# Attention with forgetting gates and a SwiGLU block on one core: first loads in another order, two PSUM banks kept for the first products with v, and all units planned anew

## The chip, the cores and the metric

The kernel runs on one core of a Trainium2 chip. The metric is the device time of one execution in microseconds (us); the time before is the median of three runs, 419.12 us. A trace of one further execution shows what each engine did: PE (TensorE, matmuls; PEld are its weight loads), DVE (VectorE), ACT (ScalarE), POOL (GpSimd) and SP (SyncE, which here only issues DMAs). ACT and POOL issue DMAs too, each on a queue of its own.

## What is computed

Eight batches with eight heads, 576 positions, head size 64. Attention with a decay from cumulated logarithms of the gates f, causal, and then a gated feed-forward block on the joined heads (4608 tokens, 512 wide, inner width 1536). Cut to what matters:

```python
scores = q @ k.T / sqrt(64)
cum = cumsum(log(clip(f, 1e-4, 1)), axis=-1)
scores = where(causal, -1e9, scores + cum[:, :, :, None] - cum[:, :, None, :])
attn = softmax(scores) @ v
x = attn.transpose(0, 2, 1, 3).reshape(4608, 512)
g = x @ w_gate
out = (g * sigmoid(g) * (x @ w_val)) @ w_out
```

q, k, v, f and the weights come as float32 from HBM; matmuls run in bfloat16, sums in float32.

## The kernel before

**Units.** Two heads that lie beside each other make a pair: 32 pairs, four to a batch, 0 to 3 for batch 0. A pair's nine blocks of 64 queries fall into group 0 (blocks 0 to 3) and group 1 (blocks 4 to 8). A unit is a pair and a group, written 10 for pair 1, group 0. `HEAD` (L266) orders the first eight units: 00 10 20 30 11 01 31 21.

**What one unit does.** `scores` (L581): matmuls of a pair's q (tile qz, which is the stationary operand) with its k (kt) into banks of the pool sp (two banks), with a small mask matmul (L598). DVE adds the cumulated gates (tile cb) and takes the row minimum in the same pass (L622), into one of four t tiles. ACT takes exp with row sums (L642). DVE inverts the sums (L658 or ACT's L656, then L660), POOL, or ACT in the early units, scales (L678, tile pk). For pairs 0 to 7 PE transposes pk (L708), and DVE or ACT copy the result to pT (L713); later pairs use a DMA transpose. `weighted` (L716) multiplies pT with v (L734, "PV") into a bank of the pool tx (two banks), and `spread` copies that to the token-major operand xT (L758).

**q and k.** They are loaded as f32 rows, cast to bf16 (tiles qb, kb), transposed on PE into a bank of the same pool tx (L546; later pairs L467), and copied to qz and kt (L559, L561). For pairs 0 to 3 this is done in parts: part A holds the first 256 positions, which is all that group 0 needs, part B the other 320. `parts` (L486) makes one load group for two pairs: k A, q A and k B for pairs 0 and 1 together, the same for pairs 2 and 3, and q B for each pair. `load_parts` (L493) issues a group as two DMAs where it holds two pairs. Part A of pairs 0 and 1 is issued by ACT (L507), all else by SP.

**Gates of the attention.** The 64 rows of f are loaded as one tile (`gates`, L365): DVE clips (L370), ACT takes Ln (L372), DVE scans (L373). The result goes to HBM as cum_f (L382), and each pair's rows are read back from it, copied to 64 partitions (cb). For the first parts of pairs 0 to 3 and the second part of pair 0 a matmul with a 0/1 matrix does the copying instead (`select`, L389, PE's L395, copied by DVE or ACT at L400). A dummy activation (L384) makes ACT load the table that holds exp.

**The feed-forward block.** Tokens are taken in tiles of 256, 256, seven of 512, 256, 128 and 128. `gate` (L801): matmuls of xT with w_gate and w_val into banks of the pool gv (four banks, also used for the transposes of pk, the selects and the output), ACT's tanh (L822), two products on DVE (L824, L827). `project` (L830): matmuls with w_out (L844), a copy (L851) and the store (L856). A gate unit needs xT of all four pairs of its batch. POOL issues the loads of the weights in 11 pieces (L791, L795): gate and val in columns 0 to 255, 256 to 511, 512 to 1023, 1024 to 1535, then w_out in three.

**What sets the order.** The kernel records each operation with the engines that may run it, an assumed duration, the tiles it reads and writes and a priority. `Plan.order` (L63) is a list scheduler that runs when the kernel is built: it takes again and again the operation that can start first by its own clock, breaking ties by priority, and gives it an engine and a buffer. Its result is one fixed order for every engine's queue; on the chip each queue runs in that order and waits where data or a buffer isn't ready. So an assumed duration, or a wait that only the planner knows (`after`), changes nothing but the order, the engine and the buffer. `COLD` (L17) is the planner's time until which it doubles PE's durations. `STARTUP` (L265) lists the loads of the start in their order: f9 is f, p0 and p2 are parts A of two pairs, k and q parts B, c the rows of cum_f, v01 chunk 1 of batch 0's v, wg0 the piece of w_gate that begins at column 0 (numbers in blocks of 128), p4 and up whole pairs. Each load waits in the plan for the one `AHEAD` places before it, POOL's also for the one `BEHIND` places before. `NUDGE` (L269) moves the priorities of single units: a are attention units, f gate tiles, o output tiles, q preparations of a pair, v loads of v.

Of the kernel before, what the change touches and what calls it, by code (L numbers as in the profile page):

```python
# [11 lines left out]
ALU = mybir.AluOpType  # L12
# [1 line left out]

BIG = 1.0e9
HUGE = 3.0e38
COLD = 25000  # L17
SLOW = 1.03


# [179 lines left out]
def kernel(  # L200
# [11 lines left out]
    nc = tc.nc  # L212
    B, H, S, D = q.shape
# [36 lines left out]
    NHALF = 4  # L250
    NSELA = 4
    NSEL = 1
    CUT = QB * (HI[0] + 1)
    MOST = (("p", 1), ("o", 2), ("f", 3))
    AHEAD = 10
    BEHIND = 6
    BOTH = 8
    LATER = {"DVE": 100}
# [3 lines left out]
    SOON = 8  # L262
    BACK = 4
    CBACK = 5
    STARTUP = "p0 f9 k0 p2 wv0 wg0 c0 v01 q1 q0 wv2 wg2 c1 v02 v00 k2 v04 c3 q2 wv4 v03 wg4 q3 c2 p4 v11 c4 wg8 wv8 c5 v14 p5 v13 v12 p6 c7 v10 c6 wo0 wo4 wo8 p7"  # L265
    HEAD = "00 10 20 30 11 01 31 21"  # L266


    NUDGE = "a5.0:-2 a8.0:1 a13.0:-1 a15.0:-2 a17.0:-2 a18.0:1.5 a22.0:2.5 a23.0:-1 a25.1:-1 a26.1:-1.5 f1:-2 f5:9 f7:0.5 o3:-4.5 o4:-0.5 o6:-8 o7:-3 q8:-2 q13:-3.5 q20:-2 q23:2 q25:4 q26:3.5 q30:-2"  # L269

    WAIT = ""
    ORDER = [(int(u[0]), int(u[1])) for u in HEAD.split()]
# [7 lines left out]
    pl = Plan()  # L280
# [79 lines left out]

    fall = f.rearrange("b h s -> (b h) s")

    evacs, loads, sums = [], {}, {}

    def gates(key, parts, np_, prio):  # L365
        x = lambda: pl.buf(key)[0:np_, :]
        for n, (a, z, src) in enumerate(parts):
            loads["f", key, n] = pl.op({"SP": 600}, lambda e, a=a, z=z, src=src: nc.sync.dma_start(out=pl.buf(key)[a:z, :], in_=src),
                                       (), [(key, 0)] + [key] * (n == 0), prio + n * .01, dma=570)
        pl.op({"DVE": 460}, lambda e: nc.vector.tensor_scalar(x(), x(), 1.0e-4, 1.0, op0=ALU.max, op1=ALU.min),  # L370
              [(key, 0)], [(key, 1)], prio, holds=[key])
        pl.op({"ACT": 690}, lambda e: nc.scalar.activation(x(), x(), AF.Ln), [(key, 1)], [(key, 2)], prio, holds=[key])  # L372
        pl.op({"DVE": 1350}, lambda e: nc.vector.tensor_tensor_scan(x(), tiny[0:np_, 0:1].to_broadcast((np_, S)), x(), 0.0, ALU.mult, ALU.add),  # L373
              [(key, 2), "tiny"], [(key, 3)], prio, holds=[key])
# [118 lines left out]
    def load_parts(p):  # L493
        b, hp = divmod(p, NPB)
        pl.key(("cb", p), "cb", p)
        for name, x, a, z, r, n in parts(p):
            fk = (name + "f", p, x)
            pl.key(fk, name + "f")
            m = (z - a) // r

            def load(e, fk=fk, src=(k if name == "k" else q), a=a, z=z, r=r, n=n, m=m):
                for u in range(n):
                    h0 = 2 * (hp + u)
                    (nc.scalar if e == "ACT" else nc.sync).dma_start(
                        out=pl.buf(fk)[m * u:m * u + m, :, 0:r * D],
                        in_=src[b, h0:h0 + 2, a:z].rearrange("h (p r) d -> p h (r d)", r=r))
            loads[name, p, x] = pl.op({"ACT" if p == 0 and x == "A" else "SP": 550 * n}, load, (), [fk], -99 + 3 * p, dma=n * (z - a) * 2)  # L507
        for x, a, z, sel in (("A", 0, CUT, NSELA), ("B", CUT, S, NSEL)):
            if p < sel:
                select(p, x, a, z)  # L510
                continue
            for h in range(2):
                loads["cb", p, x, h] = pl.op({"SP": 600}, lambda e, h=h, a=a, z=z: nc.sync.dma_start(
                    out=pl.buf(("cb", p))[64 * h:64 * h + 64, a:z],
                    in_=cum_dram[2 * p + h:2 * p + h + 1, a:z].to_broadcast((64, z - a))),
                    ["cum_dram"], [(("cb", p), x)], -98.5 + 3 * p, dma=z - a, holds=[("cb", p)])

    def prepare_parts(p):
        for name, x, a, z, r, n in parts(p):
            fk, bk, tk = (name + "f", p, x), (name + "b", p, x), ("tt", name, p, x)  # L520
            m = (z - a) // r
            pr = min(at[p + u, x == "B"] for u in range(n)) - 1 + (name == "q") * .1
            pl.key(bk, name + "b")
            pl.key(tk, "tx", line="q")

            def cast(e, name=name, fk=fk, bk=bk, r=r, w=m * n):
                src = pl.buf(fk)[0:w, :, 0:r * D].rearrange("p h (r d) -> p r h d", d=D)
                dst = pl.buf(bk)[0:w, 0:r, :, :]
                if e == "ACT":
                    nc.scalar.activation(dst, src, AF.Copy, scale=-scale if name == "q" else 1.0)  # L530
                elif name == "q":
                    eng[e].tensor_scalar(dst, src, -scale, 1.0, op0=ALU.mult, op1=ALU.mult)
                else:
                    eng[e].tensor_copy(dst, src)
            L = 2 * r * D
            o = pl.op({"POOL": L + 60, "ACT": L * .833 + 210, "DVE": L * .62 + 60}, cast, [fk], [bk], pr)
            o.bias = SPARE if p else {}
            oks = [(("kt" if name == "k" else "qz"), p + u) for u in range(n)]
            if x == "A":
                for ok in oks:  # L540
                    pl.key(ok, ok[0])

            def transpose(e, bk=bk, tk=tk, r=r, w=m * n):
                src = pl.buf(bk).rearrange("p r h d -> p r (h d)")
                for j in range(r):
                    nc.tensor.transpose(half(tk)[:, w * j:w * j + w], src[0:w, j, :], ident[0:w, 0:w])  # L546
            pl.op({"PE": r * (m * n / 2.4 + 2.5)}, transpose, [bk], [tk] + (oks if x == "A" else []), pr, lat=200, holds=oks)
            for u in range(n):
                for lo, hi, h in ([(0, P, None)] if name == "k" else [(0, 64, 0), (64, 128, 1)]):
                    def evac(e, lo=lo, hi=hi, h=h, u=u, tk=tk, ok=oks[u], a=a, z=z, r=r, n=n, m=m):  # L550
                        src = half(tk)[lo:hi, 0:r * m * n]
                        if h is None:
                            src = src.rearrange("c (j u p) -> c u p j", j=r, u=n)[:, u, :, :]
                            dst = pl.buf(ok)[lo:hi, a:z].rearrange("c (p j) -> c p j", j=r)
                        else:
                            src = src.rearrange("c (j u i p) -> c u i p j", j=r, u=n, i=(z - a) // QB)[:, u, :, :, :]
                            dst = pl.buf(ok)[lo:hi, a // QB:z // QB, h, :].rearrange("c i (p j) -> c i p j", j=r)
                        if e == "ACT":
                            nc.scalar.copy(dst, src)  # L559
                        else:  # L560
                            nc.vector.tensor_copy(dst, src)  # L561
                    pl.op({"ACT": (z - a) * .85 + 125, "DVE": (z - a) * 1.15 + 90}, evac,
                          [tk] + ([("z", "qz", p + u)] if h is not None and p + u < len(pl.pools["qz"]) else []),
                          [(oks[u], x)], at[p + u, int(x == "B")] - .9, holds=[oks[u]])
# [151 lines left out]
    def weighted(p, gs):  # L716
        b, hp = divmod(p, NPB)
        keys, cost = [], 190
        for g in gs:
            pl.key(("xo", p, g), "tx", line="v")  # L720
            w = HI[g] - LO[g] + 1
            keys.append(("xo", p, g))
            cost += mm(*[QB * min(w, HI[g] - 2 * c + 1) for c in range(HI[g] // 2 + 1)])

        def mult(e):
            for g in gs:
                xo, pT, vt = pl.buf(("xo", p, g)), pl.buf(("pT", p, g)), pl.buf(("vt", b))
                w, nch = HI[g] - LO[g] + 1, HI[g] // 2 + 1
                for c in range(nch):
                    n = min(w, HI[g] - 2 * c + 1)  # L730
                    a = w * c if (g, c) != (1, 4) else NSL[g] - 1
                    for h in range(2):
                        r = slice(64 * h, 64 * h + 64)
                        nc.tensor.matmul(xo[r, 0:QB * n], vt[:, c, 2 * hp + h, :], pT[:, a:a + n, 64 * h:64 * h + 64],  # L734
                                         start=(c == 0), stop=(c == nch - 1))
        o = pl.op({"PE": cost}, mult, [("pT", p, g) for g in gs] + [("vt", b, c) for c in range(max(HI[g] for g in gs) // 2 + 1)],
              keys, at[p, gs[0]], lat=220, holds=[("vt", b)])
        for g in gs:
            spread(p, g, o)

# [129 lines left out]
    for b in range(B):  # L870
        pl.key(("vt", b), "vt")
        load_v(b)
    weights()
    line = []
    for x in STARTUP.split():
        n = int("".join(c for c in x if c.isdigit()))
# [95 lines left out]
```

## Time and profile before

| what | us |
|---|---|
| median of three runs (417.67 to 419.34) | 419.12 |
| the profiled execution, its own time | 418.96 |
| its span, first to last instruction | 417.2 |
| PE busy | 398.3 (95%) |
| DVE busy | 328.9 (79%) |
| ACT busy | 310.3 (74%) |
| POOL busy | 251.7 (60%) |
| matmuls of the gate unit, L816 | 110.6 and 109.3 |
| matmuls of the output, L844 | 104.2 |
| score matmuls, L594 and L598 | 71.9 and 48.0 |
| DVE's add with minimum, L622 | 130.4 |
| 16 DMA engines, queue of SP, share of the span | 71.1% |
| the same, queue of POOL (weights) | 7.6% |

Shares of busy time are means over the whole span. Matmuls are pipelined and their ends are modelled in the records, so the lengths of following matmuls overlap; the distance of their starts tells their pace. The mean granted TensorE clock is 0.996. The chain of waits that ended last lies on PE for 86% of the span and on DVE for 4%.

### The profile page before, as it was taken

What the parts mean: (1) busy time and instruction counts of PE and PEld (TensorE: products, weight loads), DVE (VectorE), ACT (ScalarE), POOL (GpSimd) and SP (SyncE); (2) the same over time, 40 slices, a digit from 0 to 9 for tenths busy, and PEclk for the clock granted to TensorE, in tenths of its full rate; (3) what the DMA queues carried; (4) which work ended last, traced back from release to release, by engine and by line L of the source; (5) the groups of instructions that cost most, each with busy time, mean ns of one, the idle gap of its engine ahead of it and who ended that gap; (6) DMA issues with size and microseconds to landing.
All of it is one profiled execution on the core that took longest, in us unless ns stands there. A gap on an engine that the chain in (4) does not pass through costs nothing.

```text
span 417.2 us, 9955 instructions
## 1 busy us (share of the span) xinstructions
PE 398.3 (95%) x3250; PEld 232.3 (56%) x3296; DVE 328.9 (79%) x1065; ACT 310.3 (74%) x872; POOL 251.7 (60%) x459
## 2 busy tenths in 40 slices
PE   1979999999999999999999999999999999999996
PEld 0636878665555555555555554555555444457675
DVE  5688999999998899989897797798967764565232
ACT  4798999989995999899999984798996533232221
POOL 7589698987887897976968678267773400000000
PEclk9998999999999999999999999999999999999999
DMA  9999979695999999899999999848999211000211
GB/s 183 253 210 225 190 135 252 159 234 141 200 229 215 264 218 236 203 232 222 228 234 218 240 221 223 194 116 190 221 217 186 55 37 50 25 27 25 77 52 52
DMA packets 144004, 71.83 MB, mean 172 GB/s; under 512 B 117904, under 2 KB 131728, under 8 KB 143952
## 3 DMA queue, kind: packets, MB, share of 16 engines
q1 hardware_dynamic: 137568, 65.95, 71.1%
q0 software_dynamic: 5808, 4.72, 7.6%
q10 hardware_dynamic: 576, 0.52, 0.5%
q8 instruction: 26, 0.43, 0.4%
q14 instruction: 26, 0.21, 0.3%
HBM read 46.65 MB, written 9.58 MB: 135 GB/s over the span
## 4 chain that ended last, share of the span: by engine, by line
PE 86%; DVE 4%; issue 1%; ACT 0%
PE gv L816 43%; PE gv L844 22%; PE sp L594 9%; PE tx L734 6%; PE tx L467 3%; PE sp L598 2%; PE gv L708 2%; DVE t L622 1%; DVE pT L713 1%; DVE hh L827 1%; DVE th L824 1%; DVE qz L481 1%; DVE kt L481 0%; ACT ot L851 0%; DVE tm L622 0%
## 5 line engine op out<-in xcount | busy, mean ns | idle before, releaser
L622 DVE CUSTOM_DVE_ANT_0 t<-sp,cb 128x320 f32<-128x320 f32 (+7 forms) x288 | 130.4, 475 | 12.1 <-PE sp L598 8.6
L678 POOL TENSOR_SCALAR pk<-e,lr 128x128 bf16<-128x128 f32 (+3 forms) x190 | 100.5, 533 | 61.8 <-DVE lr L660 16.5
L816 PE MATMUL gv<-xT,wg 128*128 128x512 bf16 (+2 forms) x563 | 110.6, 327 | 0.8
L816 PE MATMUL gv<-xT,wv 128*128 128x512 bf16 (+2 forms) x562 | 109.3, 324 | 0.9
L844 PE MATMUL gv<-wo,hh 128*128 128x512 bf16 (+1 forms) x425 | 104.2, 373 | 0.8
L824 DVE SCALAR_TENSOR_TENSOR th<-th,gv 128x512 f32<-128x512 f32 x108 | 73.9, 684 | 39.3 <-ACT th L822 38.3
L822 ACT ACTIVATE th<-gv 128x512 f32<-128x512 f32 x108 | 64.1, 594 | 44.0 <-PE gv L816 43.1
L642 ACT ACTIVATE e<-t,tm 128x576 f32<-128x576 f32 (+4 forms) x160 | 88.7, 556 | 8.9 <-DVE tm L622 8.3
L827 DVE TENSOR_TENSOR hh<-th,gv 128x512 bf16<-128x512 f32 x108 | 73.7, 685 | 8.7 <-PE gv L816 4.9
L642 ACT ACTIVATE eo<-t,tm 128x128 f32<-128x128 f32 (+3 forms) x128 | 71.1, 556 | 4.7 <-DVE tm L622 2.9
L594 PE MATMUL sp<-kt,qz 128*128 128x448 bf16 (+6 forms) x320 | 71.9, 293 | 1.5 <-DVE tm L622 1.4
L678 POOL TENSOR_SCALAR pk<-eo,lr 128x128 bf16<-128x128 f32 (+3 forms) x127 | 67.6, 532 | 5.4 <-DVE lr L660 3.1
L816 PEld LDWEIGHTS <-wg 128*128 128x128 bf16 x576 | 49.8, 98 | 35.7
L816 PEld LDWEIGHTS <-wv 128*128 128x128 bf16 x576 | 48.9, 98 | 33.7 <-issue 0.3
L844 PEld LDWEIGHTS <-hh 128*128 128x128 bf16 x444 | 39.9, 98 | 39.0
L598 PE MATMUL sp<-mask,ident 128*128 128x64 bf16 x288 | 48.0, 197 | 0.0
L594 PEld LDWEIGHTS <-qz 128*128 128x128 bf16 x320 | 30.9, 100 | 20.9 <-DVE tm L622 0.9
L851 ACT ACTIVATE ot<-gv 128x512 f32<-128x512 f32 (+1 forms) x31 | 17.9, 580 | 27.1 <-PE gv L844 26.2
L598 PEld LDWEIGHTS <-ident 128*128 128x128 bf16 x288 | 27.2, 100 | 12.6 <-issue 1.9
L734 PE MATMUL tx<-pT,vt 128*64 128x320 bf16 (+4 forms) x448 | 29.6, 266 | 1.9 <-DVE pT L713 1.3
L451 POOL TENSOR_SCALAR qb<-qf 72x1024 bf16<-72x1024 f32 x28 | 29.1, 1041 | 3.1 <-DMA qf<-in_q_dram 2.0
L642 ACT ACTIVATION_READ_ACCUMULATOR e<-t,tm 128x1 f32 x160 | 30.6, 192 | 0.0
(69 smaller groups left out, 389.0 us busy)
## 6 DMA issues: line engine op xcount, KB each, us to landing
out_dram<-ot SPq DMA_DIRECT2D x35, 256.0 KB
vf<-in_v_dram SPq DMA_DIRECT2D x32, 256.0 KB
cb<-cum_f SPq DMA_DIRECT2D x56, 144.0 KB
kf<-in_k_dram SPq DMA_DIRECT2D x28, 288.0 KB
qf<-in_q_dram SPq DMA_DIRECT2D x28, 288.0 KB
wo<-in_moe_w_out_dram POOLq DMA_DIRECT2D x3, 512.0 KB, 10.8
vf<-in_v_dram SPq DMA_DIRECT2D x8, 128.0 KB
wv<-in_moe_w_val_dram POOLq DMA_DIRECT2D x2, 512.0 KB, 8.4
```

The source lines that it names most:

```text
L451: eng[e].tensor_scalar(dst, src, -scale, 1.0, op0=ALU.mult, op1=ALU.mult)
L594: nc.tensor.matmul(sp[:, o:o + z - a], qz[:, i, :, :].rearrange("p h r -> p (h r)"), kt[:, a:z], start=True, stop=not last or p >= MFROM)
L598: nc.tensor.matmul(sp[:, o - QB:o], ident, mask, start=False, stop=True)
L622: nc.vector.tensor_tensor_reduce(out=pl.buf(tk)[:, a:z], in0=pl.buf(sk)[:, o:o + z - a], in1=pl.buf(("cm", p))[:, i, :] if own else pl.buf ...
L642: nc.scalar.activation(pl.buf(ek)[:, :L], pl.buf(tk)[:, :L], AF.Exp, bias=pl.buf(("tm", p, g))[:, 0, i:i + 1], scale=-1.0, accum_out=pl.bu ...
L678: eng[e].tensor_scalar(dst, src, r, 1.0, op0=ALU.mult, op1=ALU.mult)
L734: nc.tensor.matmul(xo[r, 0:QB * n], vt[:, c, 2 * hp + h, :], pT[:, a:a + n, 64 * h:64 * h + 64], start=(c == 0), stop=(c == nch - 1))
L816: nc.tensor.matmul(pl.buf(bk)[:, j * n:j * n + n], wt[:, ko, fc * P:fc * P + P], xT[:, ko, x0:x0 + n], start=ko == 0, stop=ko == KD - 1)
L822: pl.op({"ACT": 487}, lambda e, u=u: nc.scalar.activation(pl.buf(("th", t, u)), pl.buf(("wg", t, u)), AF.Tanh, scale=0.5), [("wg", t, u)], ...
L824: pl.op({"DVE": 605}, lambda e, u=u: nc.vector.scalar_tensor_tensor(pl.buf(("th", t, u)), pl.buf(("th", t, u)), 1.0, pl.buf(("wg", t, u)), ...
L827: pl.op({"DVE": 605}, lambda e, u=u: nc.vector.tensor_mul(pl.buf(("hh", t, u)), pl.buf(("th", t, u)), pl.buf(("wv", t, u))), [("u", t, u), ...
L844: nc.tensor.matmul(pl.buf(bk)[:, 0:z - a], hh[:, (fc % nf) * n + ms * P:(fc % nf) * n + ms * P + P], wo[:, fc, a:z], start=fc == 0, stop=f ...
```

## The change

Seven edits, all in what the planner is given:

- `STARTUP`: f is listed first (it was second); p0 and p2 follow it directly, and the rest has a new order.
- Part A of q of pairs 0 and 1 is issued by SP instead of ACT; ACT keeps part A of k.
- The three transposes of parts B of pairs 2 and 3 (k of both, q of each) wait in the plan for the PV of pair 3, group 0. Those transposes and the PVs share the two tx banks.
- `AHEAD` is 9 instead of 10.
- Assumed durations: PE doubled until 31 us instead of 25; the clip of f 0.70 us instead of 0.46; an issue of a part 0.62 instead of 0.55.
- `NUDGE` is another list.

```diff
-COLD = 25000
+COLD = 31000
...
+    LASTA = 3
...
-    AHEAD = 10
+    AHEAD = 9
...
-    STARTUP = "p0 f9 k0 p2 wv0 wg0 c0 v01 q1 q0 wv2 wg2 c1 v02 v00 k2 v04 c3 q2 wv4 v03 wg4 q3 c2 p4 v11 c4 wg8 wv8 c5 v14 p5 v13 v12 p6 c7 v10 c6 wo0 wo4 wo8 p7"
+    STARTUP = "f9 p0 p2 k0 q1 wg2 v00 wv0 k2 wv2 c1 q0 wg0 v01 c3 v02 wg4 c2 v04 v03 q3 q2 wv8 p5 p4 v10 c4 wv4 c5 c0 p6 c6 wg8 c7 wo0 v14 wo8 v13 v12 p7 v11 wo4"
...
-    NUDGE = "a5.0:-2 a8.0:1 a13.0:-1 a15.0:-2 a17.0:-2 a18.0:1.5 a22.0:2.5 a23.0:-1 a25.1:-1 a26.1:-1.5 f1:-2 f5:9 f7:0.5 o3:-4.5 o4:-0.5 o6:-8 o7:-3 q8:-2 q13:-3.5 q20:-2 q23:2 q25:4 q26:3.5 q30:-2"
+    NUDGE = "a7.1:1.5 a13.1:-2 a14.0:2 a16.0:-1 a17.0:-2.5 a21.0:-2 a24.0:2 a26.0:3 f4:-1 f6:1 f8:8 o0:1 o4:-4 q2:0.5 q13:-1.5 q14:-2 q15:-4.5 q16:-4 q19:-3 q23:-3.5 q25:1.5 q27:-4 q29:-0.5 q30:-2.5 v6:2 v7:8.5"
...
-    evacs, loads, sums = [], {}, {}
+    evacs, loads, sums, lasts, heads = [], {}, {}, [], {}
...
-        pl.op({"DVE": 460}, lambda e: nc.vector.tensor_scalar(x(), x(), 1.0e-4, 1.0, op0=ALU.max, op1=ALU.min),
+        pl.op({"DVE": 700}, lambda e: nc.vector.tensor_scalar(x(), x(), 1.0e-4, 1.0, op0=ALU.max, op1=ALU.min),
...
-            loads[name, p, x] = pl.op({"ACT" if p == 0 and x == "A" else "SP": 550 * n}, load, (), [fk], -99 + 3 * p, dma=n * (z - a) * 2)
+            loads[name, p, x] = pl.op({"ACT" if (name, p, x) == ("k", 0, "A") else "SP": 620 * n}, load, (), [fk], -99 + 3 * p, dma=n * (z - a) * 2)
...
-            pl.op({"PE": r * (m * n / 2.4 + 2.5)}, transpose, [bk], [tk] + (oks if x == "A" else []), pr, lat=200, holds=oks)
+            o = pl.op({"PE": r * (m * n / 2.4 + 2.5)}, transpose, [bk], [tk] + (oks if x == "A" else []), pr, lat=200, holds=oks)
+            if x == "B" and p >= 2:
+                lasts.append(o)
...
+        heads[p, gs[0]] = o
...
+    for o in lasts:
+        o.after.append(heads[LASTA, 0])
```

The planner makes new orders of this for all five queues. Compared instruction by instruction, both programs hold the same matmuls. Apart from the order, some operations move between engines: at the start the cast of k's part A goes from ACT to DVE, the first two copies to kt from DVE to ACT, and the copies of pT of pairs 0 and 1 from DVE to ACT; exp's dummy activation stands much later in ACT's queue, so that the table load stands directly before the first exp. In SP's queue f is still the first load, followed by parts A of q (pairs 0, 1), of k and of q (pairs 2, 3), a chunk of v, and then parts B; before, f was followed by part B of k (pairs 0, 1) and parts A of pairs 2 and 3. In POOL's queue the pieces of w_gate and w_val come in the order wg2 wv0 wv2 wg0 wg4 wv8 wv4 wg8 (before: wv0 wg0 wv2 wg2 wv4 wg4 wg8 wv8). In PE's queue the first gate matmuls stand before the scores of unit 31; before, they stood after three of their banks.

## The prediction

> **What bounds the kernel now.** I began with the table of stretches (engine busy time, granted TensorE clock, DMA share); columns are stretch and length, then PE, PEld, DVE, ACT, POOL.
>
> ```profile
> 0.00:10.00 10.00, 0.87 (x5) 0.64 (x6) 5.26 (x13) 4.69 (x7) 7.43 (x33) 1.00 0.90 182
> 10.00:20.00 10.00, 10.00 (x55) 6.25 (x55) 6.06 (x28) 7.25 (x27) 5.88 (x12) 1.00 1.26 251
> 20.00:30.00 10.00, 7.76 (x77) 4.78 (x75) 8.79 (x40) 9.41 (x33) 8.85 (x19) 1.00 0.94 215
> 30.00:40.00 10.00, 8.44 (x72) 6.04 (x71) 8.74 (x32) 8.40 (x23) 9.02 (x16) 0.83 1.13 223
> 40.00:50.00 10.00, 10.00 (x126) 8.16 (x124) 9.95 (x28) 9.00 (x23) 7.19 (x11) 1.00 1.06 200
> 50.00:60.00 10.00, 9.71 (x135) 8.10 (x134) 10.00 (x34) 9.58 (x28) 7.77 (x12) 1.00 0.57 126
> ...
> 400.00:417.20 17.20, 13.90 (x147) 10.24 (x146) 4.12 (x6) 4.24 (x8) 0.00 (x0) 1.00 0.17 62
> ```
>
> From 40 us PE is full and sets the end; DVE is as full until about 72 us. PE's loss lies in the first 40 us. I measure it as time minus the work PE has done, each matmul at its pitch from full stretches (gate groups: 4x512 columns 0.86 us, 8x256 0.87; 8 transposes 0.45; ten PV matmuls 0.64). By the program's order this loss is 16.8 us at 22.7, 22.7 at 32.5, 24.8 at 41.7, 25.0 at 53, 26.9 at 109, 28.9 at 337; after the last matmul 3.2 us follow. A change of order gains only by lowering this loss: PE's matmuls are the same in both programs, 3,291 (3,250 in the records).
>
> The timelines of ACT, DVE and PE show why it starts late (start, length, in us).
>
> ```profile
> 2.28 1.34 ACTq L504 DMA_DIRECT2D qf<-in_q_dram  x2
> 6.25 0.63 ACT L530 ACTIVATE kb<-kf 128x512 bf16<-128x512 f32 x1 [1.09 <-DMA kf<-in_k_dram]
> 6.78 0.67 ACT L372 ACTIVATE t<-t 64x576 f32<-64x576 f32 x1
> 8.61 1.28 ACT L384 ACT_TABLE_LOAD   x1
> 14.67 0.51 ACT L642 ACTIVATE eo<-t,tm 128x256 f32<-128x256 f32 x1 [0.16 <-DVE tm L622]
> ```
>
> ```profile
> 4.00 0.80 DVE L370 TENSOR_SCALAR t<-t 64x576 f32<-64x576 f32 x1
> 8.25 1.34 DVE L373 TENSOR_TENSOR_SCAN t<-tiny,t 64x576 f32<-64x576 f32 x1
> ```
>
> ```profile
> 9.74 1.19 PE L395 MATMUL gv<-t,one 64*128 64x256 f32 x2 [2.20 <-DVE t L373]
> 13.40 0.40 PE L594 MATMUL sp<-kt,qz 128*128 128x256 bf16 x1
> 32.52 0.36 PE L734 MATMUL tx<-pT,vt 128*64 128x256 bf16 x4 [0.20 <-DVE qz L561]
> 34.30 1.91 PE L816 MATMUL gv<-xT,wg 128*128 128x256 bf16 x8
> ```
>
> f is clipped at 4.80, but its Ln stands behind a cast of k that waits for its load until 6.25. The first gate matmuls need PV of pairs 0 to 3; pair 3's comes at 32.52 though its pT copy (DVE, 28.64 + 0.56) ends at 29.2: second-part transposes of q and k at 28.93 and 29.52 hold both tx banks. In finer stretches the clock fell then:
>
> ```profile
> 31.00:32.00 1.00, 0.36 (x3) 0.20 (x3) 0.97 (x7) 0.98 (x3) 0.46 (x1) 1.00 1.23 197
> 33.00:34.00 1.00, 0.89 (x5) 0.35 (x5) 1.00 (x6) 1.00 (x5) 0.99 (x2) 0.53 1.10 274
> 35.00:36.00 1.00, 1.00 (x6) 0.67 (x5) 0.95 (x7) 0.00 (x0) 1.00 (x3) 0.50 1.03 215
> ```
>
> **The change, step by step (before -> after).** I follow the changed instruction order with the durations of these rows.
>
> *Head.* ACT issues only k's first part (0.74 + 1.51); q's goes onto SP's queue behind f, so ACT is 1.34 us freer. The k cast moves to DVE, where no row has its form: at least 0.41 (DVE's 128x256 cast), at most 0.80 (its 64x576 L370); 0.55, nearer the 128x512 rows at 0.68. Ln now ends at 4.95 + 0.67 = 5.6, the scan runs behind the cast, 6.25 + 0.55 to 6.8, then 1.34, to 8.15 (was 9.59). SP's q part has f ahead of it; its landing was 7.9 when issued at 2.28, and I take 6.5. Up to 7.0 is free, since its transposes must only end before the scan. Two selects, not three, stand before the first scores: 8.3 + 2 x 1.03 = 10.4 (was 13.40).
>
> *Exp's table.* The load at 8.61 lay in ACT's wait for PE. After, exp's dummy activation (0.20) stands some 200 places later and the load right before the first exp: copy ends 10.8, plus 1.28 = 12.1, where the scores' sums are ready at 11.6. First exp 12.1 (was 14.67): 2.6 gained, 0.5 given back.
> [...]
>
> *To the second halves.* Until pair 1's first full bank, ACT has 11.1 us of work (16 exps 7.0; k cast 0.74; pT copies 2 x 0.8; others 1.8), so its first exp there comes at 23.3 (was 26.19). DVE has 9.7 us from 11.2 on plus 1.3 of waits (for a select, for the reduce of exp's sums, for a cast): 22.2 (was 24.79). Lead 2.6 to 2.9.
>
> *Banks kept.* The three late transposes follow pair 3's PV. The five banks of pair 1, 5.0 us on DVE with its copies, lead to pT at 27.2, PV at 27.3 (was 32.52), x at 28.1. In PE's queue four score banks of pair 0 and nine transposes stand between; DVE frees the sp banks for them until 29.7. First gate matmul 29.9 (was 34.30), with 0.6 us less PE work before it: loss 20.0 against 23.8. Density there is about 0.45 work per us; before, 0.47 in 26.6:30.0 kept the clock and 0.25 in 30.0:33.4 lost it for 3.4 us, which cost 1.1 (23.8 -> 24.9). I take it that the clock holds.
> [...]
>
> *Given back.* From 30 on the new order has fewer gate groups between score banks, and PE waits for DVE: three second-part copies (0.49 + 0.98) stand before the bank that pair 3's scores need (PE idle 0.8), then th, ACT's pT copy and POOL's q cast (at 41.5) hold it 0.4 to 0.65 at a time, nine waits with 4.6 us in all. Pair 4's scores are out at 45.4 with 21.0 us of work done: loss 24.4, against 25.0 in the same place. PE's lead is 0.6; DVE's at equal work is 3.4 (32.2 us done at 40.0; before, 30.8 at 42.0).
>
> *Later.* Between 53 and 109 before loses 1.9 more, where DVE and PE are both full. With DVE 3.4 ahead most of that should go: I take 1.4 (bounds -0.5, if the new order waits elsewhere, and 1.9). After 109 before loses 2.0 in 230 us and then the tail; units are nudged anew there, cost taken as 0, bounds -1 and +1. The ot copies, kt and qz copies that change between ACT and DVE lie under PE.
>
> *Loads.* SP's queue: its order stalls on casts at 22.2 (DVE, q's second part) and 26.1 (POOL), and serves q and k of pair 4 at about 24 to 27 (was 23.9 to 29.5); no one waits for them before 38. Weights: the seventh piece (val columns 512 to 1023) is issued at 36.8 behind pair 0's normalizing on POOL; needed at 45.4. Landings of 512 KB took 6.6, 8.7, 10.3 and 10.2:
>
> ```profile
> wg<-in_moe_w_gate_dram POOLq DMA_DIRECT2D x1, 512.0 KB, 10.3
> wv<-in_moe_w_val_dram POOLq DMA_DIRECT2D x1, 512.0 KB, 10.2
> ```
>
> so it lands between 43.4 and 47.1. SP has nothing new to issue from about 34.5 to 38.5, as in the stretch of the 6.6: I take 8.5, no stall.
>
> **Sum.** 0.6 + 1.4 = 2.0 us off the profiled execution's own 418.96 (span 417.2 + 1.76): 416.9. That execution lies 0.16 below the median of three, 419.12.
>
> **Rivals.**
> 1. *The waits of 30 to 45 aren't there.* They rest on my following DVE's order by hand; if ACT or POOL finish earlier, PE keeps the loss of the first gate. Gain 23.8 + 1.1 - 20.0 = 4.9 less about 0.5: 414.5. For it: DVE's lead of 3.4. Against: DVE's queue order is fixed, and second-part copies stand ahead of banks.
> 2. *Weights late (slower).* Seventh piece at 10.3: lands 47.1, PE stands 1.7; the eighth, issued at about 41.7 behind three casts, lands 52.0, needed at about 50.4: 1.6 more. A PE this idle loses the clock once more (1.1 to 1.7). 3.3 + 1.4 - 2.0 = 2.7 slower: 421.6. It decides from landings above about 9 us. For it: the last two of before took 10.3 and 10.2. Against: SP's pause.
> 3. *DVE's lead is not converted*: only 0.6 is left, 418.4; the nudges wait elsewhere.
> 4. *The head doesn't move*: f was already first on SP. If k lands at 8 rather than 6.25, the scan ends where it did and all leads shrink by 1.7: 418.6. Against: k is still ACT's first issue.
>
> **How the numbers follow.** What a measurement of this kernel can tell from no change is about 0.5%, 2.1 us: below 417.0 is faster, above 421.2 slower. Forecast 0.42 (own range 415.7 to 418.1, a little over half under 417.0), rival 1 0.27, rival 2 0.15 (half above 421.2), rivals 3 and 4 together 0.16. Faster: 0.25 + 0.27 = 0.52; slower 0.08 + 0.03 for what I don't see in the later order = 0.11; the rest, 0.37, within. Range 413.6 to 420.4: leaves out the best part of rival 1 and most of rival 2.
>
> **What would show it.** After's scan starts at 6.8, first scores at 10.4, a table load of 1.28 right before the first exp, pair 3's PV near 27, first gate near 30 and no clock of 0.5 after it; PE waits between 30 and 45 that sum to some 4 us; wv's seventh piece issued near 37. I am wrong if the first gate matmul comes after 32, if PE stands for a weight landing, or if PE's idle time past 100 us grows by over 1 us.

## The result, and the profile after

The changed kernel took 421.8 us (median of four runs, 421.70 to 421.98) beside 418.86 for the kernel before on the same chip: ratio 1.0068, 95% interval 1.0045 to 1.0092. It is slower; the forecast was 416.9 with a range to 420.4. Two later measurements on other chips gave 420.17 (ratio 1.0028, 1.0008 to 1.0048), which lies inside that range, and 421.16 (1.0047, 1.0020 to 1.0074): always slower, by 0.3 to 0.7%. One of the twelve executions behind 421.16 was in the slow state; without it the median is 421.00. The profiled execution took 421.98 with a span of 420.2.

The table of stretches of the changed kernel, columns as before:

```profile
0.00:10.00 10.00, 3.26 (x14) 2.03 (x15) 5.47 (x13) 4.93 (x11) 7.27 (x33) 1.00 0.75 170
20.00:30.00 10.00, 6.85 (x69) 4.17 (x68) 9.34 (x37) 8.76 (x29) 8.83 (x19) 0.91 1.20 213
30.00:40.00 10.00, 9.46 (x101) 7.57 (x100) 9.75 (x32) 9.66 (x27) 7.32 (x13) 0.92 1.14 228
40.00:50.00 10.00, 7.71 (x90) 5.65 (x89) 8.32 (x26) 7.87 (x20) 7.53 (x11) 0.83 1.16 222
50.00:60.00 10.00, 10.00 (x129) 8.44 (x126) 9.36 (x29) 9.85 (x23) 8.11 (x13) 1.00 1.08 186
```

Work moved forward into the first 10 and the fourth 10 us, but from 40 to 50 PE is busy 7.71 of 10 where it was full before, and DVE 8.32 instead of 9.95: a hole in which both stand. The granted clock is 0.83 there. DMA moves 186 GB/s from 50 to 60, before 126: loads that used to be done are still running.

The head, in the timelines of DVE, PE and ACT:

```profile
5.84 0.54 DVE L535 CAST kb<-kf 128x512 bf16<-128x512 f32 x1 [1.04 <-DMA kf<-in_k_dram]
6.31 1.33 DVE L374 TENSOR_TENSOR_SCAN t<-tiny,t 64x576 f32<-64x576 f32 x1
...
9.77 0.39 PE L597 MATMUL sp<-kt,qz 128*128 128x256 bf16 x1
...
10.26 1.28 ACT L645 ACT_TABLE_LOAD   x1
11.55 0.51 ACT L645 ACTIVATE eo<-t,tm 128x256 f32<-128x256 f32 x1
...
14.93 0.74 ACT L531 ACTIVATE kb<-kf 128x640 bf16<-128x640 f32 x1 [1.62 <-DMA kf<-in_k_dram]
...
28.27 0.53 PE L737 MATMUL tx<-pT,vt 128*64 128x256 bf16 x4 [0.51 <-DVE pT L716]
31.28 1.24 PE L820 MATMUL gv<-xT,wg 128*128 128x256 bf16 x8
```

Scan, first scores (13.40 before) and first exp (14.67) come 0.5 to 0.6 us earlier than forecast; the gate unit starts at 31.28 (34.30 before, 29.9 forecast). Then PE meets these waits, and the clock falls:

```profile
42.91 0.43 PE L468 MATMUL tx<-ident,qb 72*128 72x72 bf16 x8 [1.07 <-POOL qb L452]
44.64 0.30 PE L597 MATMUL sp<-kt,qz 128*128 128x320 bf16 x1 [0.60 <-DVE tm L625]
45.43 1.23 PE L737 MATMUL tx<-pT,vt 128*64 128x320 bf16 x10 [0.47 <-DVE qz L482]
47.54 1.63 PE L820 MATMUL gv<-xT,wv 128*128 128x256 bf16 x8
```

```profile
44.00:45.00 1.00, 0.36 (x4) 0.20 (x2) 0.97 (x3) 1.00 (x4) 1.00 (x3) 1.00 1.04 256
46.00:47.00 1.00, 1.00 (x10) 0.52 (x7) 1.00 (x3) 0.45 (x3) 1.00 (x3) 0.50 1.03 214
48.00:49.00 1.00, 1.00 (x7) 0.75 (x6) 0.57 (x4) 0.48 (x3) 0.15 (x1) 0.62 1.15 255
```

The measure of the prediction, time minus PE work at full pitch (called loss below), taken where so much work is done (us). Second and third profiles come from the experiments; e5 and e16 are one kernel with an edit, told below.

| PE work | before | before, 2nd | after | after, 2nd (e14) | after, 3rd (e15) | e5 | e16 |
|---|---|---|---|---|---|---|---|
| 10 | 23.06 | 23.12 | 21.18 | 20.20 | 21.57 | 20.56 | 20.99 |
| 15 | 24.67 | 24.71 | 22.38 | 21.48 | 22.80 | 21.85 | 22.27 |
| 26 | 24.89 | 24.93 | 26.82 | 26.34 | 27.74 | 24.38 | 28.63 |
| 62 | 26.57 | 26.61 | 27.80 | 27.32 | 29.01 | 25.38 | 29.61 |
| 167 | 27.72 | 27.76 | 28.99 | 28.54 | 30.22 | 26.56 | 30.80 |
| last gate groups | 28.90 | 28.94 | 31.69 | 29.89 | 32.42 | 28.67 | 33.56 |
| own time | 418.96 | 419.00 | 421.98 | 420.13 | 422.72 | 418.99 | 423.82 |

After leads by 1.9 to 3.2 us at 15 us of work. It loses 4.4 to 4.9 up to 26, where before loses 0.2, and is behind. Up to 62 it regains 0.4 to 0.7, and from there it loses 2.6 to 3.9 where before loses 2.3. Before's two profiles agree within 0.06 us everywhere; after's three don't.

### The profile page after: what moved, and what is told of

Same layout as the page of the kernel before. It is cut to its first block, busy times and chain, and to the rows that moved or that the text cites. A ratio compares the mean times of both kernels' runs of the same rounds, so it can differ in the third digit from the quotient of the medians.

```text
span 420.2 us, 9973 instructions
## 1 busy us (share of the span) xinstructions
PE 399.3 (95%) x3247; PEld 233.4 (56%) x3296; DVE 327.5 (78%) x1055; ACT 314.2 (75%) x883; POOL 250.4 (60%) x458
## 4 chain that ended last, share of the span: by engine, by line
PE 72%; DMA 4%; issue 1%; POOL 0%; ACT 0%
PE gv L820 39%; PE gv L848 18%; PE sp L597 7%; PE tx L737 4%; DMA pT<-pk 4%; PE tx L468 2%; PE sp L601 1%; POOL kb L454 0%; PE gv L711 0%; ACT ot L855 0%
## 5 line engine op out<-in xcount | busy, mean ns | idle before, releaser
L848 PE MATMUL gv<-wo,hh 128*128 128x512 bf16 (+1 forms) x419 | 102.2, 373 | 1.2
L645 ACT ACTIVATE e<-t,tm 128x448 f32<-128x448 f32 (+4 forms) x160 | 88.8, 557 | 7.1 <-DVE tm L625 6.7
L597 PE MATMUL sp<-kt,qz 128*128 128x192 bf16 (+7 forms) x318 | 73.6, 295 | 2.9 <-DVE tm L625 2.7
L681 POOL TENSOR_SCALAR pk<-eo,lr 128x384 bf16<-128x384 f32 (+3 forms) x127 | 67.6, 532 | 13.0 <-DVE lr L663 7.5
L645 ACT ACTIVATE eo<-t,tm 128x384 f32<-128x384 f32 (+3 forms) x128 | 71.1, 557 | 3.1 <-DVE tm L625 1.7
L855 ACT ACTIVATE ot<-gv 128x512 f32<-128x512 f32 (+1 forms) x35 | 20.2, 581 | 31.4 <-PE gv L848 31.3
```

Source lines behind the costliest of these rows:

```text
L597: nc.tensor.matmul(sp[:, o:o + z - a], qz[:, i, :, :].rearrange("p h r -> p (h r)"), kt[:, a:z], start=True, stop=not last or p >= MFROM)
L645: nc.scalar.activation(pl.buf(ek)[:, :L], pl.buf(tk)[:, :L], AF.Exp, bias=pl.buf(("tm", p, g))[:, 0, i:i + 1], scale=-1.0, accum_out=pl.bu ...
L681: eng[e].tensor_scalar(dst, src, r, 1.0, op0=ALU.mult, op1=ALU.mult)
L848: nc.tensor.matmul(pl.buf(bk)[:, 0:z - a], hh[:, (fc % nf) * n + ms * P:(fc % nf) * n + ms * P + P], wo[:, fc, a:z], start=fc == 0, stop=f ...
```

## The experiments

All use the 2,698 operations of the changed program. In all but e4 and e14 the list of which operation is issued next, on which engine, is given instead of planned (buffers are then taken in that order); in e4 the planner itself runs, and e14 is the changed kernel as it is:

```diff
-        for o in pl.order():
+        for o in replay(pl, unpack(SEQ)):
```

One comparison needed no run. With the three edges of `lasts` taken out of the changed program, the planner's order is the same on all five engines, operation by operation. Those edges are no part of the result; that the transposes come behind pair 3's PV follows from the other edits alone.

**Start against later order (e1 to e4).** e1: changed order up to 55 us of planned time, then before's. e2: the mirror image. e3: before's to 200 us, then the changed one. e4: the changed program with before's `NUDGE`.

> The instructions that the changed program orders ahead of 55 us (by its own planner's time) in the changed order and on the changed engines, all others in the order and on the engines of before; same work. Theory (the new start loses about 1.0 us net by 56 us: 27.4 against 26.5 us of PE time lost at equal work; the new later order loses 2.0 more): 418.9 + 1.0 = 419.9. Rival A (the start does all of it, the later growth only follows from how it leaves the queues and the clock): 421.8. Rival B (the later order does all of it, the start's lag is made up under an order with slack): 418.9.

> The mirror image: the first 55 us in the order of before, all that follows in the changed order. Theory: 418.9 + 2.0 = 420.9, with before's one clock drop and first gate at 34.3. Rival A (start does all): 418.9. Rival B (later order does all): 421.8.

> Order of before up to 200 us, the changed order from there. Between 200 us and the end the changed kernel loses 1.3 to 1.5 us more than before at equal work (1.5 behind at 193 us, 3.0 at the end). Theory (the later order loses by itself, at the late transposes of p and the late casts of k): 418.9 + 1.4 = 420.3, with matmuls that wait for pT and for kb in 200 to 290 us. Rival A (those waits are an echo of the start): 418.9.

> The changed kernel with before's line of nudges (NUDGE); the first 26 us of its order stay as they are. Theory: the start's loss stays (about 1 us by 56 us), the later order is a third one; if the new nudges are what costs the 2.0 us, 419.9. Rival A: 421.8. Rival C (nudges fit only the start that they were made for): worse than the changed kernel, above 422.

Measured: 425.46 (ratio 1.0170, 1.0144 to 1.0197), 422.51 (1.0104, 1.0071 to 1.0136), 422.84 (1.0118, 1.0092 to 1.0145), 424.82 (1.0141, 1.0095 to 1.0188). The theory missed in all four, by 1.6 to 5.6 us; e4 alone came out as one of its rivals had it (C: above 422). In e1 to e3 the engines aren't where the second order expects them, and 3 to 4 us are lost where the orders meet (e1: 27.3 to 31.1 between 32 and 42 us of work; e3: 29.2 to 32.9 between 167 and 193). Their times say nothing on the split, the losses behind the seam do: from 42 us of work to the last gate groups e1 loses 2.94 in before's order (before: 2.95), e2 4.65 in the changed one (after's first profile: 4.69). e4 has no seam, and e1 and e4 show what the hole at 47 us is:

```profile
48.22 1.03 PE L820 MATMUL gv<-xT,wv 128*128 128x256 bf16 x4 [3.25 <-DMA wv<-in_moe_w_val_dram]
```

That is e4, on PE, where the clock is also 0.50 from 47 to 50.5; in e1, with after's start and a clock of 1.00 throughout, the same group stands 1.34 us for the same piece.

**The weight piece, q's cast, the transpose (e5 to e8).**

```diff
 POOL, e5
+L795 wv pieces 4 to 7   (behind the cast of v at 32.2)
 L681 pk of pair 0, four tiles
-L795 wv pieces 4 to 7
 L681 pk of pair 0, two tiles
+L795 wg pieces 8 to 11
 L454 kb, kb; L452 qb
-L795 wg pieces 8 to 11
 SP, e6
-L424 qf of pair 5   (at 28.1)
+L424 qf of pair 4
 ...
-L424 qf of pair 4   (at 33.0)
+L424 qf of pair 5
 SP, e8
-L431 cb, four loads
 L694 pT of pair 23
 L860 out
 L424 kf, qf of pair 26
+L431 cb, four loads
```

e6 has qb ahead of the second kb on POOL too; e7 is both.

> The changed kernel with its order kept but for two of POOL's issues: the seventh weight piece (val columns 512 to 1023) moved from behind pair 0's normalizing to ahead of it (32.8 instead of 37.7 us), the eighth (gate columns 1024 to 1535) from behind the casts of k and q to the old place of the seventh. Theory W (in the stretch from 45 to 49 us the changed kernel stands on the seventh piece: its gate group starts at 47.5 to 48.5 in every execution, with a lost clock before it or with a visible wait): the group no longer waits and the loss at 26 us of PE work falls from 26.8 to about 25.6; time 421.8 - 1.2 = 420.6. Rival K (the clock's fall at 45 us is the cost, the piece isn't): no change, 421.8. Rival Q (q's late cast at 41.8 us sets it all): no change.

> The changed kernel with pair 4's q loaded in pair 5's place (SP 28.1 instead of 33.0 us) and pair 5's in pair 4's, and pair 4's q cast by POOL ahead of pair 5's k instead of behind it. The wait of PE for that cast at 41.8 us (1.07) should go. Rival Q: the loss at 26 us of work falls by about 1.1 and the time to 420.7. Theory W: PE only reaches the seventh weight piece sooner and stands for it instead; loss at 26 us unchanged within 0.3, time 421.6.

> Both edits together (weights and pair 4's q early). Theory W: both waits go, loss at 26 us of work about 24.6, 2.2 less than the changed kernel; time 419.6. Rival K (clock): 421.8 less at most 1.1. If the loss only moves further along (a wait for DVE's sums), 421.

> The changed kernel with four of SP's loads (the cumulative gates of pairs 26 and 27, 144 KB each) moved from ahead of the DMA transpose at 250.8 us to behind it and the loads of pair 26's k and q that follow. The transpose stood 7.33 us there against 4.4 in other places. Theory L (the later order's loss comes from loads queued right ahead of a transpose): the transpose takes about 5, k of pair 26 is issued about 255 instead of 258.9, its cast on POOL comes before 261 instead of 263.8, and PE's wait of 0.60 at 264.6 is gone; loss between 232 and 245 us of work falls from 0.78 to 0.1, time 421.1. Rival (POOL is too full for this cast whatever the loads do): wait stays, 421.8.

e5: 419.51 (1.0028, 1.0008 to 1.0048); the gate group no longer waits, and PE is full from 45 us on:

```profile
45.70 1.04 PE L820 MATMUL gv<-xT,wv 128*128 128x256 bf16 x8
```

Loss at 26 us of work 24.38, more taken out than theory W had; the changed kernel's three profiles have 26.34 to 27.74 there. e6: 420.15 (1.0045, 1.0026 to 1.0065): the wait for q's cast is gone and PE stands 0.60 for the weight piece, which had hidden behind it; loss 26.08, close to the lowest of those three, so no gain is shown. e7: 419.69 (1.0024, 1.0006 to 1.0043), loss 24.70: q early adds nothing to the weights. The changed kernel wasn't measured on this chip; e14, on another, has the ratio of e5. e8: 420.24 (1.0032, 1.0013 to 1.0050). Its SP queue (first two lines the changed kernel, last two e8):

```profile
250.80 7.33 SPq L694 DMA_TRANSPOSE pT<-pk  x1
...
258.86 0.37 SPq L424 DMA_DIRECT2D kf<-in_k_dram  x1
```

```profile
248.11 6.56 SPq L694 DMA_TRANSPOSE pT<-pk  x1
...
255.39 0.38 SPq L424 DMA_DIRECT2D kf<-in_k_dram  x1
```

k of pair 26 is issued 3.5 us earlier, its cast starts at 258.82 instead of 263.77, and of the wait in the changed kernel

```profile
264.64 0.43 PE L468 MATMUL tx<-ident,kb 96*128 96x96 bf16 x6 [0.60 <-POOL kb L454]
```

nothing is left (loss from 232 to 245 us of work 0.00, was 0.78). But the edit isn't shown to be the reason. In e14 and e15, which keep the four loads in their place, the same transpose holds SP 7.19 and 7.16 us, the cast starts at 259.71 and 262.32, and PE doesn't wait either (loss there at most 0.02). What e8 shows is a transpose that is shorter by some 0.6 us and a k that is issued earlier; whether PE waits for it differs between executions of one order.

**Nudges without a seam, and the second parts (e9 to e11).** For e9 and e10 the planner itself went on from the given first 60 us, so nothing meets; e9 has e5's early weights in them. e11 is e5's order and:

```diff
 SP
-L778 vf, first rows
 L505 kf, qf, kf (second parts)
+L778 vf, first rows
 POOL
-L795 wg, wv (first pieces)
 L535 kb; L533 qb
-L782 vt
+L795 wg, wv (first pieces)
 ...
+L782 vt (behind pair 0's normalizing)
```

> The changed order for the first 60 us with the two weight pieces early (as in the run that had that alone: 419.5, loss 24.4 at 26 us of PE work, 28.7 at the end); from 60 us on the planner goes on by its own rules with before's nudges in place of the new ones, so there is no seam where two orders meet. From 62 us of work to the end before's order loses 2.3, the changed one 3.6 to 3.9. Theory L (the new nudges place loads ahead of transposes and late casts, 1.0 us at 211 to 228 and 0.8 at 265): the loss after 62 us of work is about 2.3, the time 419.5 - 1.4 = 418.1. Rival N (any order planned behind this start loses as much): 419.5. Rival A (start leaves the queues worse, the nudges don't matter): 419.5 to 420.

> The mirror image: the first 60 us as in before, from there the planner goes on with the new nudges. Theory L: loss after 62 us of work about 3.9 instead of 2.3, time 419.1 + 1.6 = 420.7, with a PE wait for pT or for a k cast in 200 to 290 us. Rival N or A: 419.1.

> The kernel with the two weight pieces early, and in the first 16 us the second parts of k and q of pairs 0 to 2 loaded ahead of the first rows of v on SP, the first two weight pieces issued by POOL behind the casts at 9 us instead of at 5.2, and the cast of v behind pair 0's normalizing. Theory S (the first gate matmul came at 31.3 instead of 29.9 because these second parts landed late: the cast of k at 14.9 us waited 1.6 for its load): that cast starts about 13.3, pair 3's PV comes near 27.3 and the first gate near 30; loss at 10 us of work 19.6 to 20.2 instead of 20.6 to 21.2. Whether it reaches the end: if DVE's sums hold PE between 31 and 46 us all the same (0.7 to 2 us of waits there in every run so far), the loss at 26 us of work is 24.0 to 24.4 and the time 419.3; if it is handed on in full, 418.5. Rival: weights that start later are late again at 47 us, over 420.

e9: 420.92 (1.0062, 1.0036 to 1.0088), e10: 421.69 (1.0068, 1.0050 to 1.0087). From 62 us of work on they lose 4.6 and 4.9: theory L holds for e10, with a wait at the very place where the changed kernel has it (pair 20, 227.91 there with 0.41), but not for e9, where before's nudges put a transpose late behind the other start (in e4, where PE was 5 us behind, the same nudges lost only 2.2). Lines of e9, then e10:

```profile
130.98 0.71 PE L737 MATMUL tx<-pT,vt 128*64 128x320 bf16 x10 [1.90 <-DMA pT<-pk]
```

```profile
73.42 0.81 PE L848 MATMUL gv<-wo,hh 128*128 128x512 bf16 x3 [1.24 <-DMA wo<-in_moe_w_out_dram]
229.32 0.88 PE L737 MATMUL tx<-pT,vt 128*64 128x320 bf16 x14 [1.53 <-DMA pT<-pk]
```

Both swaps cost more than either order kept whole, which is rival N's kind: nudges fit the start that they were planned behind. One profile of each is all that this rests on. e11: 419.66 (1.0035, 1.0013 to 1.0057). The cast that waited 1.62 us at 14.93 now runs at 12.85, and the first gate matmul stays at 30.71 (30.62 in e5). So theory S, by which the gate would come near 30, falls; what the late second parts do set is told below.

**Do the parts add up? (e12 to e17).** e12: e5's edit, e8's, and one output store behind pair 20's transpose. e13: also this on DVE, at 44 us:

```diff
+L482 qz of pair 4
 L625 t, a bank of 512
-L482 qz of pair 4
```

e14, e15: the changed kernel itself. e16: e5 again, on e15's chip. e17: before's own order.

> The changed order with the seventh and eighth weight piece early, the four loads behind the transpose at 250 us and one output store behind pair 20's transpose at 220 us. Theory (the changed kernel's 2.8 us of extra loss are 2.4 for the weight piece and 0.8 to 1.3 for two late transposes' sake, less what it gained): loss at 26 us of PE work 24.4, 28.0 at the end; 418.99 - 0.7 = 418.3 for an execution, 418.7 as median beside 419 for before. Rival (transposes come late at another place instead): 419.5 as with the weights alone.

> The same and DVE's copy of pair 4's q from behind a score bank to ahead of it (at 44 us), where DVE stands 0.5 us for PE and PE then 0.47 for that copy. Theory D (what is left of the lead between 31 and 46 us goes into waits for DVE): the wait of 0.47 goes, loss at 26 us of work 23.9 to 24.1, median 418.3. Rival: the bank behind the copy comes later by as much, 418.7.

> The changed kernel itself beside the others on one chip, so that the sizes don't hang on two chips. Theory: 421.8, 2.5 to 3 over before, and 2.3 over the weights-early run; loss 26.8 to 27.5 at 26 us of work, either by a wait of 1.3 to 1.7 for the seventh weight piece or by a lost clock just ahead of it. Rival (the difference to before was mostly the first chip's): within 1.5 of before.

> The changed kernel's order once more, on the same chip as the next two. Its losses are to be compared: at 26 us of PE work 26.3 to 26.8 by the theory, and from 62 us of work to the end 2.6 (as in its second profile) to 3.9 (as in its first).

> The changed kernel with the seventh and eighth weight piece early, beside the changed kernel on one chip. Theory W: the 2.0 us that this takes out of the loss at 26 us of work reach the end, median 1.5 to 2.3 lower. Rival H (handed on: PE that is ahead meets the late transposes, casts and sums of 200 to 270 us instead; the loss from 62 us of work on was 3.3 and 3.6 in the two profiles with weights early, 2.6 in the changed kernel's second): median lower by at most 0.7, a profile with the loss at 26 us 2 lower and that from 62 us on 0.7 to 1.3 higher.

> The order of before, unaltered, for a second profile of it on the same chip. Its loss at 26 us of work was 24.9 with a lost clock at 33 to 36 us and 23.0 in a run that shared its first 55 us and lost none there. Theory: 23.0 to 24.9 there, and 2.3 to 2.5 from 62 us of work to the end, in any execution, 419.0. If the later loss is 3 or more here too, the later part of the changed kernel's loss is chance and not order.

e12: 420.44 (1.0033, 1.0015 to 1.0050), no better than e14's 420.17 on the same chip, though its profile has 2.2 less loss at 26 us of work: transposes are in time, and a sum of DVE is late instead (0.38 at 226.05). e13: 422.29 (1.0065, 1.0042 to 1.0088): the copy ahead of the bank makes PE stand 1.32 us for that bank at 45.37, where 0.27 and 0.47 were. e14's rival came true: it lies 1.16 above before on its chip, and a good part of the 2.9 of the first measurement isn't there. Its profile shows the hole without a lost clock, and pair 4's scores out at 45.92:

```profile
45.92 0.19 PE L601 MATMUL sp<-mask,ident 128*128 128x64 bf16 x1
47.65 1.05 PE L820 MATMUL gv<-xT,wv 128*128 128x256 bf16 x8 [1.54 <-DMA wv<-in_moe_w_val_dram]
```

e15: 421.00, e16: 419.77 (1.0028, 1.0000 to 1.0056) on one chip: early weights bring 1.2 us there, but the two intervals against before overlap. e16's profile fell on its slowest execution (423.82) and bears out neither theory W nor rival H: the loss at 26 us of work is 28.63, above e15's 27.74. The casts of k and q of pair 4 are late, and then the clock falls, with no weights awaited (the seventh piece, issued at 33.1, landed in 12.8, at 45.9; its group starts at 49.35).

```profile
41.51 0.43 PE L468 MATMUL tx<-ident,kb 96*128 96x96 bf16 x6 [1.04 <-POOL kb L454]
```

```profile
43.50:50.50 7.00, 5.74 (x41) 3.86 (x42) 4.39 (x14) 4.95 (x15) 4.96 (x8) 0.52 1.05 202
```

From 44.03 to 50.82 PE does 3.0 us of work, so 3.8 are lost; 0.7 of them are waits for DVE, and about 3 the slower clock.

e17: 419.13, ratio 0.9996 (0.9975 to 1.0016), losses as in the table. No version beat the kernel before.

## Why the prediction was wrong

**Head, exp's table: right.** Scan, scores and exp came 0.5 to 0.6 us better than worked out; the load took 1.28 as in its row (10.26 to 11.54), and the first exp starts at 11.55.

**To the second halves: waits of DVE sized too small.** First gate 31.28 instead of 29.9, loss at it 21.4 instead of 20.0. It isn't the edges (the order is the same without them), and DVE's work was listed rightly: from 11.20 to pair 1's first full bank it is busy 9.29 us (9.7 in the prediction). But it waits 2.8 there, not 1.3, and 1.48 of this is for a copy of q that ACT makes only behind k's late cast (14.93 above). So the bank came at 23.32, not at 22.2:

```profile
15.96 0.43 DVE L564 COPY qz<-tx 64x256 bf16<-64x256 bf16 x1 [1.48 <-ACT qz L562]
23.32 0.67 DVE L625 CUSTOM_DVE_ANT_0 t<-sp,cb 128x512 f32<-128x512 f32 x1
```

In e14 the load of k landed sooner, and the gate was 0.4 us behind the forecast:

```profile
14.22 0.74 ACT L531 ACTIVATE kb<-kf 128x640 bf16<-128x640 f32 x1 [0.90 <-DMA kf<-in_k_dram]
30.26 1.03 PE L820 MATMUL gv<-xT,wg 128*128 128x256 bf16 x8
```

In the ten profiles that share this start (the changed kernel's three, e5 to e8, e12, e13, e16) the cast starts between 14.22 and 15.46 and the gate follows it by 16.0 to 16.4 us. So between executions the landing of that load sets the gate. e11 has the cast at 12.85 and the gate still at 30.71, so with an earlier load another wait takes over.

**The clock: wrong, but covered here by the late weights.** It fell twice (0.5 at 28.4 to 31.8 and 45.3 to 48.7). The second fall costs 1.5 in after; in e14 it doesn't come and PE stands 1.54 for the weight piece, 1.70 of loss in place of it. From 15 to 26 us of work the changed kernel's three profiles lose 4.4, 4.9 and 4.9, where the first and third lost the clock and the second didn't. With the weights early it isn't covered any more: about 3 us in e16. The same instructions lost the clock in two executions (after and e15) and kept it in two others: the 128x512 scores behind pair 3's PV took 0.61 at 29.26 in after, 0.58 at 29.73 in e15 and 0.38 at 28.50 in e14, and e1's start and e14 show 1.00 in every us from 44 to 49, though PE is busy for only 0.12 (e1, 47 to 48) and 0.11 (e14, 46 to 47) of one of them. That the clock holds was an estimate from the densities of one execution of before; what decides it isn't shown.

**Given back: right in size.** I had 4.4 us of waits and a loss of 24.4 when pair 4's scores are out; e14 shows 24.5 there, after's first profile 26.1 with 0.9 of lost clock in it. They are late sums (0.37, 0.60), the late cast of q (1.07) and copy (0.47), in the places named.

**Loads: the step that failed.** "I take 8.5, no stall" for the seventh weight piece. It was issued at 37.70 (36.8 forecast), landed in 9.5, 47.2, and in e14 and e1 not before 47.6 and 48.4. In e14 the 24.5 at pair 4's scores and 1.7 of stall make 26.2 (26.3 at 26 us of work), and the forecast lead of 0.6 is a lag of 1.4. This is rival 2's first part, 1.7 us. Its second (the eighth piece, 1.6) doesn't show as a wait of PE in any of after's three profiles, so it is luck that rival 2's 421.6 lies near the first 421.80. With the piece early, e5's profile leads by 0.5 at 26 us of work, as forecast, and by 1.2 at 62; it ends level with before all the same (418.99 and 418.96), so this step alone doesn't make up the 416.9. What I overlooked: by 28 us the new order had moved 5.56 MB where before had moved 6.09, by 44 us 9.15 against 9.56 (summed from the GB/s of 4 us windows). SP's pause from 34.5 to 38.5 came (35.7 to 40.5), but what it had issued before was still being moved (215 GB/s over all queues, 0.89 of the 1.03 MB on SP's). That this made the piece late isn't shown: a piece of this size took 10.2 in before, too. In e16 POOL stood 1.1 us for one of SP's loads ahead of the cast of k once the weights went out earlier; e5, with the same edit, has no such wait.

**Later: half right, then wrong.** Of the 1.4 that DVE's lead should win back between 53 and 109 us, 0.4 to 0.7 came by 62 us of work (89 us); DVE's lead itself went into the hole at 40 to 50. "After 109, cost taken as 0, bounds -1 and +1" was 0.2 to 1.6 in after's profiles (62 us of work to the end: 2.6 to 3.9, before 2.3): ten loads queued right ahead of the transposes of pairs 19 and 23, which then held SP for 8.67 and 7.33 us where the median is 4.4, and PE's product and a cast behind them came late. In e14 the same two took 7.61 and 7.19 and neither wait is there, so long transposes cost time only in some executions. In e5, with the weights early, this part costs 1.0, which is the lead that it had at 62 us of work less what was left at the end. The term taken as 0 is the second step that failed.

**What stays open.** How much of each part reaches the end. Beside e14's 26.34, early weights took 2.0 and 2.2 out of the loss at 26 us of work in e5 and e12, but e16's profile has more loss than e15's. They took 1.2 out of the median on one chip and nothing, with two more edits, on another, and every version with them was still measured slower than before. What else keeps the later order from its forecast wasn't found.

## What to carry to other kernels

When loads are put in a new order, add up the bytes moved by the time of each deadline and cost the last piece at the slowest landing that the profile shows, not at a middle one: here 8.5 was taken, before's rows had up to 10.3, and 9.5 to 10.7 came, which turned no stall into one of up to 1.7 us. A wait found in a trace may stand ahead of another that is due at the same time (q's cast, the lost clock and the weight piece here); take each away alone before it is given a size. A wait that is gone behind an edit may be gone in another execution of the unedited kernel too (e8 beside e14 and e15); profile that one more than once. Fine corrections to a plan seem to fit the start they were made behind (e9, e10).

## What was not expected of the hardware

- A DMA transpose of 25 tiles of 128x128 held SP's queue 3.7 to 8.7 us in one program (median 4.4); the two longest follow some ten loads of 144 to 288 KB. With four of ten loads taken from ahead of it, the one near 250 us took 6.56; in the changed kernel's three profiles it took 7.33, 7.19 and 7.16.
- On one chip before's executions lie between 417.0 and 421.2 (24 runs) and the changed kernel's between 418.7 and 423.0 (12 runs), a width of some 4 us for both. Of the twelve the one of 418.7 has a mean granted clock of 0.986 and one of 420.7 has 1.000: the mean clock doesn't order them.
